# Attention scores computed transposed and turned in 32x32 blocks on VectorE, in batches 1 to 7 of a three-part kernel

## The chip, the core and the metric

The kernel runs on one core of a Trainium2 chip. The metric is device time in microseconds (us) of one execution; the time of the kernel before is the median of three runs. TensorE does the matrix products, VectorE (DVE in the rows) and ScalarE (ACT) the work on elements, GpSimd (POOL) some reductions and stores, SyncE (SP) issues most transfers.

## The reference

An attention against 32 memory slots for each head, and two feed-forward layers one after the other. Eight batches of 8 heads, 576 tokens, head size 64; then 4608 tokens of width 512, inner width 2048.

```python
a = softmax(phi, axis=2)                              # over the 576 tokens
k_m = einsum('bhsm,bhsd->bhmd', a, k)
v_m = einsum('bhsm,bhsd->bhmd', a, v)
attn = softmax(q @ k_m.transpose / sqrt(64), axis=-1) # over the 32 slots
x = (attn @ v_m), heads side by side                  # 4608 x 512
h = x @ w_in;   x = (h * sigmoid(h)) @ w_out
h = x @ w_in2;  x = elu(h) @ w_out2
```

## The kernel before

The kernel has two halves in time. In the first, batch after batch of 576 tokens goes through attention and the first layer; in the second, nine blocks of 512 tokens go through the second layer. Products of the two layers run in float16, each operand split into a high and a low half (`split_hi` on ScalarE, `split_lo` on VectorE, lines 170 to 177) and multiplied in three terms (`mm3`). Everything up to the attention weights is float32.

For one batch, `plan_mem` makes `k_m` and `v_m` (tiles `phi`, `eT`, `es`, `kvp`, `kvTp`, `kT`), `plan_u` multiplies `v_m` into the first weight matrix (`up`, `u`), and `plan_attn` makes the attention weights in three pieces j: 256, 256 and 64 tokens. For a piece of 256 tokens `scores` (L776) issues 16 matmuls with 64 tokens of `q` as weights and 64 columns of `kT` moving, tokens on the partitions of PSUM tile `sc`; `tile_position` puts them on the left or right 64 columns of the array. `att_max` and `att_sub` (VectorE, L793, L800) subtract the maximum over 32 slots, `att_exp` (ScalarE) takes the exponential, `att_sum` and `att_mul` (VectorE) divide by the sum. `att_T` (TensorE, L829) transposes the weights into PSUM tile `aTp`, slots on the partitions, and `att_split` brings them as a high and a low half into `aT`. The sixteen products of in1 (`plan_in1`, PSUM tile `ph` from `aT` and `u`) read `aT`; the seven products of out1 (`plan_out1`, `ph` from `T` and `w1s`) read operand splits `T` that VectorE and ScalarE make from the activations `h` (`plan_moving`). Conversions of the second layer's weights (`quad`, `raw`, `hl_q`) are spread over batches 2 to 7.

Batch 0 runs in an order written out by hand (`FIRST`); from batch 1 on a planner (`Plan`) sets the order: each step has an engine, an estimated cost, a rank or due time and the steps that it depends on, and each engine's list is filled by rank and readiness. Each engine then works through its list strictly in order. Attention of batch n + 1 is planned beside in1 and out1 of batch n. `sc` and `aTp` share a ring of two PSUM tiles (`A = "a", 2`), the weights `att` have two SBUF tiles.

Of the kernel before, what the change touches and what calls it, by code (L numbers as in the profile page):

```python
# [10 lines left out]
F32 = mybir.dt.float32  # L11
# [3 lines left out]
AF = mybir.ActivationFunctionType  # L15
ALU = mybir.AluOpType
AX = mybir.AxisListType
PSUM = bass.MemoryType.PSUM

P = 128  # L20
B, H, S, D, M = 8, 8, 576, 64, 32
DM, DFF = 512, 2048
NG = 2
NP = 4
NC = 5
TAIL = 64
# [51 lines left out]
def act(n, scaled=True):  # L78

    return (0.25 if scaled else 0.19) + n / 1165  # L80


def dve(n, fast=False):

    return 0.155 + n / (1920 if fast else 915)
# [7 lines left out]
def attn_moe_moe(ctx: ExitStack, tc: tile.TileContext, qT, phiT, kvm, kvt, w1i, w1o, w2i, w2o, out):  # L93
# [24 lines left out]
    def a_tile(shape, name, tag="a"):  # L118

        k = turn[0] % 4  # L120
        turn[0] += turn[1]
        if turn[1]:
            tag = "aauc"[k]
        return ps_a.tile(shape, F32, tag=tag, name=name, bufs=2 if tag == "a" else 1)
# [4 lines left out]
    def small(name, n=1):  # L129
        return sml.tile([P, n], F32, tag=f"s{n}", name=name, bufs={1: 10, 16: 6}.get(n, 2))  # L130
# [4 lines left out]
    def tt(out, a, b, op):  # L135
        nc.vector.tensor_tensor(out=out, in0=a, in1=b, op=op)  # L136
# [635 lines left out]
    def tokens(j):  # L772

        return (P, 2) if j < 2 else (TAIL, 1)

    def scores(b, j):  # L776
        z = st[b]
        r, n = tokens(j)
        ps = z["sc", j] = a_tile([P, 2, H, M], "sc")
        for c in range(2 * n if j < 2 else 1):  # L780
            t0 = 256 * j + 64 * c
            o = 64 * (c % 2)
            for p in range(NP):
                nc.tensor.matmul(  # L784
                    ps[o:o + 64, c // 2, 2 * p:2 * p + 2],
                    z["q", p][:, t0:t0 + 64],
                    z["kT"][:, p // 2, 64 * (p % 2):64 * (p % 2) + 64],
                    start=True,
                    stop=True,
                    tile_position=(0, o),  # L790
                )

    def att_max(b, j):  # L793
        z = st[b]
        r, n = tokens(j)
        sc = z["sc", j][:r, :n].rearrange("p n h m -> p (n h) m")
        z["smx", j] = small("smx", 16)
        nc.vector.tensor_reduce(out=z["smx", j][:r, :n * H], in_=sc, axis=AX.X, op=ALU.max)

    def att_sub(b, j):  # L800
        z = st[b]
        r, n = tokens(j)
        k = n * H
        sc = z.pop(("sc", j))[:r, :n].rearrange("p n h m -> p (n h) m")
        a = z["att", j] = two.tile([P, 16, M], F32, tag="att", name="att")
        tt(a[:r, :k], sc, z.pop(("smx", j))[:r, :k].unsqueeze(2).to_broadcast([r, k, M]), ALU.subtract)

    def att_exp(b, j):
        r, n = tokens(j)
        a = st[b]["att", j][:r, :n * H]  # L810
        nc.scalar.activation(out=a, in_=a, func=AF.Exp, scale=float(1.0 / np.sqrt(D)))

    def att_sum(b, j):
        r, n = tokens(j)
        k = n * H
        aa = st[b]["att", j][:r, :k]
        s1, s2 = small("ss1", 16), small("ss2", 16)
        st[b]["ss3", j] = small("ss3", 16)
        nc.vector.tensor_reduce(out=s1[:r, :k], in_=aa, axis=AX.X, op=ALU.add)
        nc.vector.tensor_scalar_add(s2[:r, :k], s1[:r, :k], 1e-9)  # L820
        nc.vector.reciprocal(st[b]["ss3", j][:r, :k], s2[:r, :k])

    def att_mul(b, j):
        r, n = tokens(j)
        k = n * H
        aa = st[b]["att", j][:r, :k]
        tt(aa, aa, st[b].pop(("ss3", j))[:r, :k].unsqueeze(2).to_broadcast([r, k, M]), ALU.mult)

    def att_T(b, j):  # L829
        z = st[b]  # L830
        r, n = tokens(j)
        a = z.pop(("att", j)).rearrange("p (n g h) m -> p n g (h m)", n=2, g=NG)
        ps = z["aTp", j] = a_tile([P, NG, 256], "aTp")
        for g in range(NG):
            for c in range(n):
                nc.tensor.transpose(ps[:, g, P * c:P * c + r], a[:r, c, g], ident[:r, :r])  # L836

    def att_split(b, j, lo):
        z = st[b]
        r, n = tokens(j)  # L840
        if j == 0 and not lo:
            z["aT"] = big.tile([P, NG, S], F32, tag="aT", name=f"aT{b}", bufs=2) if b == 0 else big.tile(
                [P, 2, NG, S], F16, tag="aT", name=f"aT{b}", bufs=2)
        t = slice(256 * j, 256 * j + n * r)
        ps = z["aTp", j][:, :, :n * r]
        if b == 0:
            copy(f"A0{j}", z["aT"][:, :, t], ps)
        elif not lo:
            split_hi(z["aT"][:, 0, :, t], ps, SA)
        else:  # L850
            split_lo(z["aT"][:, 1, :, t], z["aT"][:, 0, :, t], ps, SA)
# [121 lines left out]
    def plan_attn(pl, n, r, mem, after):  # L973


        A = "a", 2

        def on(eng, cost, fn, deps):
            return pl.add(eng, cost, r, fn, deps)

        qs, q_frees = [], []
        for p in range(NP):
            if n > 1:
                qs.append(pl.load(295, r - 290, lambda p=p: load_q(n, p), pl.ring("q", NP), QLATE))
            q_frees.append(pl.take("q", qs[-1]) if n > 1 else pl.rings["q"][p][1])
        aT, exps = [], []
        for j in range(3):
            rows, w = tokens(j)
            k = 256 * w
            sc = on("PE", 1.8 if j < 2 else 0.5, lambda j=j: scores(n, j), [mem["kT"]] + qs + pl.ring(*A))  # L990
            free = pl.take("a", sc)
            mem["kT_free"].append(sc)
            for f in q_frees:
                f.append(sc)
            mx = on("DVE", dve(k), lambda j=j: att_max(n, j), [sc])
            t = on("DVE", dve(k), lambda j=j: att_sub(n, j), [mx] + pl.ring("att", 2))
            a_free = pl.take("att", t)
            free.append(t)
            t = on("ACT", act(k, False), lambda j=j: att_exp(n, j), [t] + after)
            exps.append(t)  # L1000
            t = on("DVE", dve(k) + 0.45, lambda j=j: att_sum(n, j), [t])
            t = on("DVE", dve(k), lambda j=j: att_mul(n, j), [t])
            t = on("PE", 0.6 if j < 2 else 0.3, lambda j=j: att_T(n, j), [t] + pl.ring(*A))
            a_free.append(t)
            free = pl.take("a", t)
            h = on("ACT", act(k, False), lambda j=j: att_split(n, j, False), [t] + (aT or pl.ring("aT", 2)))
            if j == 0:
                aT_free = pl.take("aT", h)
            t = on("DVE", dve(k), lambda j=j: att_split(n, j, True), [h])
            free.append(t)  # L1010
            aT.append(t)
        return {"aT": aT, "exps": exps, "aT_free": aT_free, "scales": mem["scales"]}
# [850 lines left out]
```

## Time and profile before

| | |
|---|---|
| three runs | 1386.82, 1390.85, 1391.38 us; median 1390.85 |
| the profiled execution, span from first to last instruction | 1390.1 us |
| TensorE busy | 1345.9 us, 97% |
| VectorE busy | 1130.3 us, 81% |
| ScalarE busy | 948.2 us, 68% |
| batches 1 to 7 on TensorE | about 117 to 700 us |
| second layer | about 700 to 1390 us |

The profile gives, for one execution, each engine's instructions with their start and length. Matmuls overlap in the array, so the length of a row of matmuls is longer than the time to the next row's start; what a step costs TensorE is read from the distance of starts. PE is TensorE's matmuls, PEld its weight loads. A float32 matmul leaves two records.

### The profile page before, as it was taken

To read this page: it belongs to the slowest core of one execution; us is meant where nothing else is said; L and a number is where in the kernel's file an instruction comes from. 1 tells how busy PE (TensorE), PEld (TensorE's weight loads), DVE (VectorE), ACT (ScalarE), POOL (GpSimd) and SP (SyncE) were. 2 spreads that over 40 slices of the span, in tenths; PEclk is the share of its full clock that TensorE was granted. 3 is DMA by queue.
4 is the path that set the end of the run, shared out by engine and by line. 5 is a ranking of instruction groups with operands and counts; after the bars stand their busy time and mean duration, and the time that the engine had idled before them with its cause. 6 is when DMAs were issued, how large, how long until landed. Compare 5 with 4: busy or idle time off the path is not lost.

```text
span 1390.1 us, 28629 instructions
## 1 busy us (share of the span) xinstructions
PE 1345.9 (97%) x12048; PEld 1091.0 (78%) x12048; DVE 1130.3 (81%) x1753; ACT 948.2 (68%) x1357; POOL 53.2 (4%) x85
## 2 busy tenths in 40 slices
PE   4999999999999999999999999999999999999998
PEld 2676677776767767676787888888888888888887
DVE  6888888796998979797869787888888787879784
ACT  3666784967868685786658675758676676768672
POOL 0000100010010000001000000000000000000000
PEclk8999999999999999999999999999999999999999
DMA  9556777368576647745394232333333241514220
GB/s 368 178 180 214 261 271 255 131 224 283 179 244 238 228 167 250 262 141 215 119 368 154 82 129 82 122 99 100 107 104 118 71 151 43 170 51 141 81 95 31
DMA packets 68800, 233.06 MB, mean 168 GB/s; under 512 B 9024, under 2 KB 15168, under 8 KB 64064
## 3 DMA queue, kind: packets, MB, share of 16 engines
q1 hardware_dynamic: 60288, 199.78, 42.4%
q0 software_dynamic: 8384, 31.46, 5.8%
q8 instruction: 94, 1.54, 0.5%
q14 instruction: 34, 0.28, 0.1%
HBM read 186.12 MB, written 40.89 MB: 163 GB/s over the span
## 4 chain that ended last, share of the span: by engine, by line
PE 84%; DMA 5%; issue 4%; DVE 3%; ACT 3%; POOL 0%; SPq 0%; ACTq 0%; POOLq 0%; DVEq 0%
PE ph L1029 28%; PE o L1029 23%; PE h2A L1029 13%; PE h2D L1029 9%; PE ph L1078 3%; DMA wi<-w2is 2%; PE up L869 2%; PE ph L1036 2%; PE sc L784 2%; PE kvp L688 1%; DMA kv<-in_kvm 1%; DMA w2is<-hl_q 1%; PE eT L665 0%; DMA raw<-in_w1o 0%; PE aTp L836 0%
## 5 line engine op out<-in xcount | busy, mean ns | idle before, releaser
L1029 PE MATMUL o<-t,wq 128*128 128x256 f16 x3024 | 358.3, 273 | 0.1
L1029 PEld LDWEIGHTS <-wi 128*128 128x128 f16 x3024 | 295.1, 98 | 46.4 <-DMA wi<-w2is 9.3
L1029 PEld LDWEIGHTS <-wq 128*128 128x128 f16 x3024 | 295.7, 98 | 34.7 <-issue 0.3
L1029 PE MATMUL ph<-T,w1s 128*128 128x288 f16 x2352 | 301.7, 287 | 0.2 <-DVE T L177 0.2
L1029 PEld LDWEIGHTS <-w1s 128*128 128x128 f16 x2352 | 225.9, 98 | 64.0 <-issue 7.7
L1029 PE MATMUL h2A<-xh,wi 128*128 128x256 f16 x1728 | 228.6, 273 | 8.9 <-DMA wi<-w2is 7.4
L1467 ACT ACTIVATE h<-h2A,inv 128x256 f32<-128x256 f32 x288 | 133.7, 468 | 141.6 <-PE h2A L1029 139.2
L1029 PE MATMUL ph<-aT,u 128*128 128x288 f16 x1344 | 176.5, 288 | 1.1 <-ACT h L1115 0.9
L177 DVE SCALAR_TENSOR_TENSOR t<-h,s_g,t 128x768 f16<-128x768 f32 (+1 forms) x144 | 163.9, 1146 | 14.2 <-ACT t L172 13.9
L1029 PE MATMUL h2D<-xh,wi 128*128 128x256 f16 x1296 | 172.9, 273 | 0.0
L1471 DVE SCALAR_TENSOR_TENSOR h<-h2D,inv,h 128x256 f32<-128x256 f32 x216 | 103.8, 482 | 81.0 <-PE h2D L1029 59.1
L1029 PEld LDWEIGHTS <-u 128*128 128x128 f16 x1344 | 127.7, 98 | 49.6 <-issue 18.4
L172 ACT ACTIVATE t<-h,s_g 128x768 f16<-128x768 f32 (+1 forms) x144 | 146.4, 1034 | 22.8 <-DVE h L136 11.5
L177 DVE SCALAR_TENSOR_TENSOR T<-h,c,T 128x1152 f16<-128x1152 f32 x98 | 137.2, 1413 | 20.0 <-ACT T L172 19.7
L136 DVE TENSOR_TENSOR h<-h 128x256 f32<-128x256 f32 (+1 forms) x302 | 129.5, 463 | 2.8
L172 ACT ACTIVATE T<-h,c 128x1152 f16<-128x1152 f32 x98 | 119.5, 1252 | 13.8 <-DVE h L136 10.3
L1115 ACT ACTIVATE h<-ph,inv 128x576 f32<-128x576 f32 x112 | 82.3, 738 | 24.1 <-PE ph L1029 23.0
L1509 DVE SCALAR_TENSOR_TENSOR h<-e,h 128x1024 f32<-128x1024 f32 x72 | 87.8, 1219 | 7.3 <-ACT e L1505 7.3
L1502 ACT ACTIVATE e<-h 128x1024 f32<-128x1024 f32 x72 | 75.5, 1049 | 8.8 <-DVE h L1471 8.8
L1505 ACT ACTIVATE e<-e 128x1024 f32<-128x1024 f32 x72 | 75.6, 1050 | 0.7
L1078 PE MATMUL ph<-h,w1o 128*128 128x288 f32 x256 | 66.5, 418 | 0.0
L136 DVE TENSOR_TENSOR h<-h,h 128x1152 f32<-128x1152 f32 x42 | 56.5, 1354 | 9.9 <-ACT h L1115 9.7
(183 smaller groups left out, 1272.5 us busy)
## 6 DMA issues: line engine op xcount, KB each, us to landing
w1s<-w1os SPq DMA_DIRECT2D x98, 512.0 KB, 4.6
wi<-w2is SPq DMA_DIRECT2D x56, 896.0 KB, 4.7
kv<-in_kvm SPq DMA_DIRECT2D x48, 256.0 KB, 5.3
q<-in_qT SPq DMA_DIRECT2D x32, 288.0 KB, 7.9
out<-ye SPq DMA_DIRECT2D x36, 256.0 KB, 2.0
raw<-in_w1i SPq DMA_DIRECT2D x8, 1024.0 KB, 11.4
raw<-in_w1o SPq DMA_DIRECT2D x8, 1024.0 KB, 4.9
raw<-in_w2i SPq DMA_DIRECT2D x8, 1024.0 KB, 6.9
```

The costliest lines, as they stand in the source:

```text
L136: nc.vector.tensor_tensor(out=out, in0=a, in1=b, op=op)
L172: nc.scalar.activation(out=hi, in_=x, func=AF.Copy, scale=s)
L177: nc.vector.scalar_tensor_tensor(out=lo, in0=x, scalar=s, in1=hi, op0=ALU.mult, op1=ALU.subtract)
L784: nc.tensor.matmul(ps[o:o + 64, c // 2, 2 * p:2 * p + 2], z["q", p][:, t0:t0 + 64], z["kT"][:, p // 2, 64 * (p % 2):64 * (p % 2) + 64], st ...
L1029: nc.tensor.matmul(o, w, x[:, c], start=first, stop=last, **how)
L1078: nc.tensor.matmul(z[d][1][t], wB[d][:, k], h[k // KQ][:, t, k % KQ], start=(k == 0), stop=(k == KF - 1))
L1115: nc.scalar.activation(out=h[m // KQ][:, :, m % KQ], in_=w.pop(m), func=AF.Silu, scale=z["inv1"][:, m // 4:m // 4 + 1])
L1467: nc.scalar.activation(out=w["x"][:, s], in_=w["A"], func=AF.Copy, scale=inv)
L1471: return pl.add("DVE", COST["add"], base, lambda: nc.vector.scalar_tensor_tensor(out=w["x"][:, s], in0=w["D"], scalar=inv, in1=w["x"][:, s ...
L1502: nc.scalar.activation(out=w["e"], in_=w["x"][:, B21:], func=AF.Relu, scale=-1.0)
L1505: nc.scalar.activation(out=w["e"], in_=w["e"], func=AF.Exp, scale=-1.0)
L1509: nc.vector.scalar_tensor_tensor(out=x, in0=w["e"], scalar=-1.0, in1=x, op0=ALU.add, op1=ALU.max)
```

## The change

Only batches 1 to 7 change. A new `scores_T` computes the scores with 64 columns of `kT` as weights and up to 256 tokens of `q` as moving columns, so that slots lie on the partitions of `sc`; the left and right half of the array alternate with every matmul. `att_turn` is one VectorE instruction that transposes every 32x32 block from PSUM into the SBUF tile `att`: tokens modulo 32 come to lie on the partitions, and the 32 slots of a head side by side. `att_sub_T`, `att_exp_T` and `att_norm_T` do the same softmax as before, now from SBUF. `att_back`, one VectorE instruction again, turns the blocks back into PSUM tile `aTp`, in which the weights have the layout that `att_T` gave them; `att_split` is as it was. The last piece of 64 tokens works on 128 partitions x 128 columns where it worked on 64 x 256. The costs that the planner is told change with the steps.

```diff
@@ -834,6 +834,62 @@
         for g in range(NG):
             for c in range(n):
                 nc.tensor.transpose(ps[:, g, P * c:P * c + r], a[:r, c, g], ident[:r, :r])
+
+    def scores_T(b, j):
+        z = st[b]
+        n = P * tokens(j)[1] if j < 2 else TAIL
+        ps = a_tile([P, NG * 256], "sc")[:, :NG * n]
+        z["sc", j] = ps
+        for g in range(NG):
+            for e in range(2):
+                o = 64 * e
+                nc.tensor.matmul(
+                    ps[o:o + 64, g * n:(g + 1) * n],
+                    z["kT"][:, g, o:o + 64],
+                    z["q", 2 * g + e][:, 256 * j:256 * j + n],
+                    start=True,
+                    stop=True,
+                    tile_position=(0, o),
+                )
+
+    def by_head(b, j):
+
+        return st[b]["att", j], st[b]["att", j].rearrange("p k m -> p (k m)")
+
+    def att_turn(b, j):
+        z = st[b]
+        ps = z.pop(("sc", j))
+        z["att", j] = two.tile([P, 16, M], F32, tag="att", name="att")[:, :ps.shape[1] // M]
+        nc.vector.transpose(out=by_head(b, j)[1], in_=ps)
+
+    def att_sub_T(b, j):
+        z = st[b]
+        a, _ = by_head(b, j)
+        k = a.shape[1]
+        mx = small("smx", 16)[:, :k]
+        nc.vector.tensor_reduce(out=mx, in_=a, axis=AX.X, op=ALU.max)
+        tt(a, a, mx.unsqueeze(2).to_broadcast([P, k, M]), ALU.subtract)
+
+    def att_exp_T(b, j):
+        a, _ = by_head(b, j)
+        nc.scalar.activation(out=a, in_=a, func=AF.Exp, scale=float(1.0 / np.sqrt(D)))
+
+    def att_norm_T(b, j):
+        a, _ = by_head(b, j)
+        k = a.shape[1]
+        s1, s2, s3 = small("ss1", 16)[:, :k], small("ss2", 16)[:, :k], small("ss3", 16)[:, :k]
+        nc.vector.tensor_reduce(out=s1, in_=a, axis=AX.X, op=ALU.add)
+        nc.vector.tensor_scalar_add(s2, s1, 1e-9)
+        nc.vector.reciprocal(s3, s2)
+        tt(a, a, s3.unsqueeze(2).to_broadcast([P, k, M]), ALU.mult)
+
+    def att_back(b, j):
+        z = st[b]
+        _, a = by_head(b, j)
+        z.pop(("att", j))
+        ps = a_tile([P, NG * 256], "aTp")[:, :a.shape[1]]
+        nc.vector.transpose(out=ps, in_=a)
+        z["aTp", j] = ps.rearrange("p (g t) -> p g t", g=NG)
 
     def att_split(b, j, lo):
         z = st[b]
@@ -986,21 +1042,20 @@
         aT, exps = [], []
         for j in range(3):
             rows, w = tokens(j)
-            k = 256 * w
-            sc = on("PE", 1.8 if j < 2 else 0.5, lambda j=j: scores(n, j), [mem["kT"]] + qs + pl.ring(*A))
+            k = 256 * w if j < 2 else P
+            sc = on("PE", 1.0 if j < 2 else 0.3, lambda j=j: scores_T(n, j), [mem["kT"]] + qs + pl.ring(*A))
             free = pl.take("a", sc)
             mem["kT_free"].append(sc)
             for f in q_frees:
                 f.append(sc)
-            mx = on("DVE", dve(k), lambda j=j: att_max(n, j), [sc])
-            t = on("DVE", dve(k), lambda j=j: att_sub(n, j), [mx] + pl.ring("att", 2))
+            t = on("DVE", dve(k), lambda j=j: att_turn(n, j), [sc] + pl.ring("att", 2))
             a_free = pl.take("att", t)
             free.append(t)
-            t = on("ACT", act(k, False), lambda j=j: att_exp(n, j), [t] + after)
+            t = on("DVE", 2 * dve(k), lambda j=j: att_sub_T(n, j), [t])
+            t = on("ACT", act(k, False), lambda j=j: att_exp_T(n, j), [t] + after)
             exps.append(t)
-            t = on("DVE", dve(k) + 0.45, lambda j=j: att_sum(n, j), [t])
-            t = on("DVE", dve(k), lambda j=j: att_mul(n, j), [t])
-            t = on("PE", 0.6 if j < 2 else 0.3, lambda j=j: att_T(n, j), [t] + pl.ring(*A))
+            t = on("DVE", 2 * dve(k) + 0.45, lambda j=j: att_norm_T(n, j), [t])
+            t = on("DVE", dve(k), lambda j=j: att_back(n, j), [t] + pl.ring(*A))
             a_free.append(t)
             free = pl.take("a", t)
             h = on("ACT", act(k, False), lambda j=j: att_split(n, j, False), [t] + (aT or pl.ring("aT", 2)))
```

The planner moves instructions accordingly. On TensorE, in batch 1, the end of the first piece of scores and the start of the second, with steps of batch 0's outer product (`ph`) between; before:

```order
L784 MATMUL sc<-kT_892,q_408 64x64
L784 MATMUL sc<-kT_892,q_410 64x64
L784 MATMUL sc<-kT_892,q_412 64x64
L784 MATMUL sc<-kT_892,q_414 64x64
L1078 MATMUL ph<-h_145,w1o_706 128x288 x16
L1078 MATMUL ph<-h_146,w1o_706 128x288 x16
L836 MATMUL aTp<-ident,att 128x128 x4
L784 MATMUL sc<-kT_892,q_408 64x64
```

and with the change, from the start of the first piece:

```order
L846 MATMUL sc<-q_408,kT_892 64x256
L846 MATMUL sc<-q_410,kT_892 64x256
L846 MATMUL sc<-q_412,kT_892 64x256
L846 MATMUL sc<-q_414,kT_892 64x256
L1133 MATMUL ph<-h_145,w1o_706 128x288 x16
L1133 MATMUL ph<-h_146,w1o_706 128x288 x16
L1133 MATMUL ph<-h_145,w1o_855 128x288 x8
L846 MATMUL sc<-q_408,kT_892 64x256
```

Sixteen matmuls became four, the transposes of `att` between the pieces are gone, and the second piece stands eight matmuls of the outer product later.

On VectorE, at the end of the attention for batch 5, where the last piece is normalised and its low half made (`aT`, 128x2x64); `u` and `y` are results of other products, `inv`, `pvw`, `rec`, `c` small constants; before:

```order
L819 TENSOR_REDUCE ss_5292<-att 64x8
L820 TENSOR_SCALAR ss_5293<-ss_5292 64x8
L821 RECIPROCAL ss_5294<-ss_5293 64x8
L177 SCALAR_TENSOR_TENSOR aT_5118<-aTp,aT_5118 128x2x256
L136 TENSOR_TENSOR att<-att,ss_5294 64x256
L1258 SCALAR_TENSOR_TENSOR y<-ph,io_4298,y 128x288 x2
L177 SCALAR_TENSOR_TENSOR u_5_5303<-up,u_5_5303 128x512
L736 TENSOR_SCALAR inv_5341<-p_w1i,p_v 128x4
L136 TENSOR_TENSOR pvw<-p_v,p_w1im 128x1
L167 RECIPROCAL rec<-pvw 128x1
L168 TENSOR_SCALAR c_5343<-rec 128x1
L177 SCALAR_TENSOR_TENSOR aT_5118<-aTp,aT_5118 128x2x64
```

and with the change, from the sum of the last piece on:

```order
L881 TENSOR_REDUCE ss_5183<-att 128x4
L882 TENSOR_SCALAR ss_5184<-ss_5183 128x4
L883 RECIPROCAL ss_5185<-ss_5184 128x4
L136 TENSOR_TENSOR att<-att,ss_5185 128x128
L177 SCALAR_TENSOR_TENSOR aT_4999<-aTp,aT_4999 128x2x256
L891 STREAM_TRANSPOSE aTp<-att 128x128
L177 SCALAR_TENSOR_TENSOR u_5_5163<-up,u_5_5163 128x512
L1313 SCALAR_TENSOR_TENSOR y<-ph,io_4215,y 128x288 x2
L177 SCALAR_TENSOR_TENSOR aT_4999<-aTp,aT_4999 128x2x64
L736 TENSOR_SCALAR inv_5227<-p_w1i,p_v 128x4
L136 TENSOR_TENSOR pvw<-p_v,p_w1im 128x1
L167 RECIPROCAL rec<-pvw 128x1
```

The second piece's `aT` and the turn back stand between the product with the reciprocal and the last piece's `aT`, and the constants now come behind that `aT`.

## Rows read from the trace of the kernel before

**Rows 1.** Busy time by stretches, out1 of batches 2 and 4: window, length, PE, PEld, DVE, ACT, POOL.

```profile
264.70:316.40 51.70, 51.70 (x499) 39.49 (x498) 48.70 (x67) 35.40 (x54) 4.97 (x6) 1.00 0.60 209
...
431.50:482.00 50.50, 50.50 (x474) 38.99 (x471) 46.92 (x67) 32.18 (x51) 2.08 (x2) 1.00 0.71 252
```

**Rows 2.** Timeline of PE, out1 of batch 4: start, length, operation, count, idle before.

```profile
446.91 1.54 PE L784 MATMUL sc<-kT,q 128*64 128x64 f32 x32
448.38 15.61 PE L1029 MATMUL ph<-T,w1s 128*128 128x288 f16 x126
...
472.09 0.60 PE L836 MATMUL aTp<-ident,att 128*128 128x128 f32 x4
472.62 0.68 PE L784 MATMUL sc<-kT,q 128*64 128x64 f32 x8
473.23 0.91 PE L1029 MATMUL ph<-T,w1s 128*128 128x288 f16 x6
...
481.29 0.34 PE L836 MATMUL aTp<-ident,att 64*128 64x64 f32 x2
481.57 0.61 PE L869 MATMUL up<-w1i_hl,vT 128*32 128x512 f16 x8
482.12 1.65 PE L1029 MATMUL ph<-aT,u 128*128 128x288 f16 x12
```

**Rows 3.** Timeline of PE: a float32 stream, and one `kvp` group with its successor.

```profile
117.32 15.79 PE L1078 MATMUL ph<-h,w1o 128*128 128x288 f32 x64
132.94 0.60 PE L836 MATMUL aTp<-ident,att 128*128 128x128 f32 x4
...
434.89 0.43 PE L688 MATMUL kvp<-kv,es 128*32 128x128 f32 x8
435.25 2.01 PE L1029 MATMUL ph<-T,w1s 128*128 128x288 f16 x15
```

**Rows 4.** Groups by form, DVE: count, then busy us, mean ns, idle before.

```profile
L329 DVE TENSOR_SCALAR quad<-quad 128x1024 f32<-128x1024 f32 x16 | 11.0, 688 | 5.1 <-ACT quad L320 5.1
...
L136 DVE TENSOR_TENSOR att<-sc,smx 128x512 f32<-128x512 f32 x16 | 11.1, 691 | 0.5
...
L798 DVE TENSOR_REDUCE smx<-sc 64x8 f32<-64x256 f32 x8 | 3.3, 412 | 1.8 <-PE sc L784 1.8
```

**Rows 5.** Timeline of DVE: low half of the third `aT` piece, batches 1 to 5, 7.

```profile
151.57 0.28 DVE L177 SCALAR_TENSOR_TENSOR aT<-aTp,aT 128x128 f16<-128x128 f32 x1
...
227.44 0.29 DVE L177 SCALAR_TENSOR_TENSOR aT<-aTp,aT 128x128 f16<-128x128 f32 x1
...
315.29 0.27 DVE L177 SCALAR_TENSOR_TENSOR aT<-aTp,aT 128x128 f16<-128x128 f32 x1
...
398.51 0.28 DVE L177 SCALAR_TENSOR_TENSOR aT<-aTp,aT 128x128 f16<-128x128 f32 x1
...
482.09 0.29 DVE L177 SCALAR_TENSOR_TENSOR aT<-aTp,aT 128x128 f16<-128x128 f32 x1
...
642.92 0.29 DVE L177 SCALAR_TENSOR_TENSOR aT<-aTp,aT 128x128 f16<-128x128 f32 x1
```

**Rows 6.** Timeline of PE: first in1 matmuls of batches 1 to 4, 7; a `kv` wait.

```profile
156.88 1.64 PE L1029 MATMUL ph<-aT,u 128*128 128x288 f16 x12
...
236.95 1.63 PE L1029 MATMUL ph<-aT,u 128*128 128x288 f16 x12
...
316.38 1.63 PE L1029 MATMUL ph<-aT,u 128*128 128x288 f16 x12
...
336.46 0.66 PE L688 MATMUL kvp<-kv,es 128*32 128x128 f32 x8 [2.47 <-DMA kv<-in_kvm]
...
402.12 1.64 PE L1029 MATMUL ph<-aT,u 128*128 128x288 f16 x12
...
644.35 3.10 PE L1029 MATMUL ph<-aT,u 128*128 128x288 f16 x24
```

## The prediction

> **What bounds the kernel now.** I read the busy time by stretches first. The kernel spends its first half on seven batches (1 to 7), each with an inner product (in1, matmuls `ph<-aT,u`) and an outer one (out1, `ph<-T,w1s`). While out1 of one batch runs, the attention of the next is made. In the two out1 stages shown TensorE is busy for all of the stretch, 51.70 of 51.70 us and 50.50 of 50.50, so TensorE's list sets the pace there; VectorE has 48.70 and 46.92 us of work in the same time and so only 3.0 and 3.6 us of idle time [rows 1]. ScalarE has 35.40 and 32.18 and is no second bound. So the reader is to see two things: a microsecond taken from TensorE in this stage is a microsecond of the kernel, as long as VectorE keeps up; and VectorE has hardly any room.
>
> Next, TensorE's list in order of time around one such stage [rows 2]. Starts follow each other without a hole, so what a piece costs is the distance to the next start and not its printed duration: scores of 256 tokens 446.91 to 448.38, 1.47 us; the last 64 tokens 472.62 to 473.23, 0.61; the transpose of attention weights 0.53 (472.09 to 472.62) and for the last piece 0.28.
>
> **The change, part by part.** *TensorE, taken away.* Each batch has two pieces of 256 tokens and one of 64: 2 x 1.47 + 0.61 + 2 x 0.53 + 0.28 = 4.89 us.
>
> *TensorE, added.* The same scores come as four matmuls for a piece (16 or 4 before), keys as weights and 256 tokens as moving columns. Each float32 matmul leaves two records in the trace, so 8 records for a piece. In a plain float32 stream 64 records of 288 columns take 117.32 to 132.94, 0.244 us each or 0.85 ns a column [rows 3]. 256 columns are thus 0.217 us: 1.74 for a piece if the two 64-column halves of the array work in turn, 0.87 if side by side. That halves can work side by side is seen in `kvp`, which changes its quarter of the array with every matmul: 8 records of 128 columns take 0.36 us [rows 3], against 0.87 in turn and 0.22 with all four side by side; it pays 0.14 over the latter. Before the change scores switch halves only after four matmuls, and gain little: 32 records of 64 columns take 1.47, in turn 1.74. After it they switch with every matmul, as `kvp` does, which is why I price them by that row: 0.87 + 0.14 = 1.01 a piece, and for the last piece, 8 x 0.054 / 2 + 0.14 = 0.36, I take 0.40, since the same size takes 0.61 today. Sum 2.42; saved per batch 4.89 - 2.42 = 2.47 us, in seven batches **17.3 us**. Bounds: no surplus, 1.96 (20.5 us in all); halves in turn, 2 x 1.74 + 0.61 = 4.09 (5.6 us in all).
>
> A rule speaks against the better price. The Trainium skill ("TensorE: Matmul & The Clock Gate", Part 3, What overlaps and what doesn't) says that matmuls start and end strictly in program order. By it the two records of one matmul, on the same half, would hold up the next, a piece would take five record times, 1.22 us, and the saving would be 14.4 us. The `kvp` row does not bear it out: five record times there would be 0.54 us, and it takes 0.36.
>
> *VectorE, added.* The trace has no turn of 32x32 blocks. The nearest rows are float32 operations on 512 columns from PSUM, 0.69 us [rows 4], so a piece of 256 tokens costs two turns (scores into SBUF, weights back into PSUM) of 0.69, and the last piece two on 128 columns, which cost 0.28 by the `aT` rows of that width [rows 5]. In return the last piece's maximum, subtraction, sum and product shrink from 256 columns on half the partitions (0.41, [rows 4]) to 128 on all, 0.28. Sum: 4 x 0.69 + 2 x 0.28 - 4 x 0.13 = **2.80 us a batch**. Bounds: half price, as an SBUF operation on 1024 columns has it (0.69, [rows 4]), 1.3; double price, 6.1. I take the middle because both reads and writes of PSUM at one column a step are what the 0.69 row shows. None of this is hidden in seven batches unless VectorE's idle time takes it in. ScalarE's exp of the last piece gets 0.1 shorter; it has room, nothing.
>
> *Moved.* The planner's list for VectorE keeps the same 14 operand splits a batch and lets weight conversions (`quad`) slip behind the attention chain; the order in the section on the change shows the end of that chain, where the third `aT` has moved ahead of the scale constants, and TensorE's list no longer holds a transpose between the pieces, so a piece of scores now waits for VectorE's turn back of the piece before, where it waited for a TensorE transpose. Queued behind a waiting turn on VectorE are the `T` splits of out1, which TensorE reads next. Loads on SP's queue are the same in number; single `q`, `kv` and `w1s` loads change places by a few. I price that at nothing, covered by three `kv` buffers; uncovered, it is one more hole like the 2.47 us wait for `kv` in batch 3 [rows 6].
>
> **What VectorE lets through.** In1 of a batch starts when the third piece of `aT` has its low half from VectorE. How long that lies before in1's first matmul is the slack: batch 1, 151.85 to 156.88, 5.0 us; batch 2, 227.73 to 236.95, 9.2; batch 3, 315.56 to 316.38, 0.8; batch 4, 3.3; batch 5, 482.38 against 482.12, none; batch 7, 643.21 to 644.35, 1.1 [rows 2, 5, 6]; batch 6 I take like 4. TensorE comes 2.47 us sooner and VectorE has 2.80 more to do, so 5.27 us must come from slack and from VectorE's 3.3 us of idle time a stage [rows 1]. That idle time is mostly waiting for ScalarE's high halves, which will be ready when VectorE is later; I let between half and all of it be used. All of it: batch 3 is short by 1.2, 5 by 2.0, 7 by 0.9, the rest by nothing, 4.1 us. Half: 2.8, 3.6, 2.5 and 0.3 each in 4 and 6, 9.5 us. TensorE waits that long, newly, for `aT` or a late `T`. Middle: 6.8.
>
> **Sum.** 17.3 - 6.8 = 10.5 us less. The profiled execution has a span of 1390.1, from which 1379.6 is left; the median of the runs is 0.75 above that span, so **1380.4 us**, with its own range 1377.6 to 1383.1. About 0.3% (4.2 us) is what a measurement of this kernel can tell from no change.
>
> **The rivals.** *A, all of it arrives:* the planner lets enough conversion work slip that `aT` and `T` are never late: 1390.85 - 17.3 = 1373.5. For it: VectorE's order puts `aT` ahead of constants; against: slack of 0.8 and none in batches 3 and 5 [rows 2, 5, 6]. 15%.
>
> *B, VectorE takes the place of TensorE:* its waits for ScalarE stay, so no idle time is used. Short by 0.3, 0, 4.5, 2.0, 5.3, 2.0 and 4.2 in the seven batches, 18.3 against 17.3: 1391.9, no difference to be told. For it: the 93 to 94% busy share [rows 1]; against: a wait for a ScalarE result shrinks when the waiting side is late. 12%.
>
> *C, the turns are dear, slower:* a 32x32 turn of 4-byte data at twice the price of a copy, 1.38 us for 512 columns, in the attention chain of every batch. Then 2.47 + 6.1 = 8.57 us must be found; half the idle used, the batches are short by 1.9, 0, 6.1, 3.6, 6.9, 3.6 and 5.8, 27.9 us in all, and the kernel takes 1390.85 + 10.6 = 1401.5. It decides from where shortages pass 17.3, at about 1.0 us a turn (five batches, 4.8 turns' worth each, 7.8 us above the 9.5). For it: no row shows a turn, and it writes PSUM, which VectorE does nowhere in this trace; against: every single-price row of this width lies at 0.69. 15%.
>
> *D, the halves do not work side by side:* the piece costs 1.74, TensorE saves 0.80 a batch, 3.60 must be found, the batches 3, 5 and 7 are short by 1.2, 1.9 and 0.9, and 5.6 - 4.0 = 1.6 us are left: 1389.2. For it: scores before gain only 0.27 of 1.74 from switching; against: `kvp`. 8%.
>
> **How the numbers follow.** The forecast gets 50%. Faster by over 0.3%: forecast and A, 0.65; within: B and D, 0.20; slower: C, 0.15. The range reaches from A to B, 1373 to 1392, and leaves out C.
>
> **What would show it.** Right: `sc` pieces of 8 records about 1.0 us from start to next start, no `aTp` matmuls in batches 1 to 7, turns near 0.69, VectorE near 50 us busy of a 49 to 51 us out1 stage, and new TensorE waits for VectorE's `aT` or `T` in batches 3, 5 and 7 of some 7 us in all. Wrong: turns of 1 us and more with waits in every batch (C), pieces of 1.7 us (D), waits of 15 us and more at single price (B), or hardly any waits (A). A new wait for `kv` loads, or a second half of the kernel that is not the same length, would be a cause that I have not priced.

## The result, and the profile after

The change made the kernel slower: median 1403.07 us of four runs (1400.63 to 1406.30) against 1390.92 of four runs of the kernel before, ratio 1.0089, 95% interval 1.0067 to 1.0111, 12 us. 1380.4 with a range of 1373 to 1392 was predicted, and the result lies outside that range. The profiled execution, the fastest of the four, has a span of 1398.9 us against 1390.1, 8.8 longer. The changed kernel's lines stand 55 or 56 below those of before: `mm3` is L1084, the addition to `y` L1313.

What the change was to do it did. In the timeline of PE (start, length, operation, count) a piece of 256 tokens takes 274.65 to 275.67, 1.02 us, and the last piece 145.38 to 145.77, 0.39 [rows 2 had 1.47 and 0.61]:

```profile
145.38 0.45 PE L846 MATMUL sc<-q,kT 128*64 128x64 f32 x8
145.77 0.61 PE L925 MATMUL up<-w1i_hl,vT 128*32 128x512 f16 x8
...
274.65 1.08 PE L846 MATMUL sc<-q,kT 128*64 128x256 f32 x8
275.67 16.71 PE L1084 MATMUL ph<-T,w1s 128*128 128x288 f16 x135
```

The turns cost what other VectorE work of their width costs, from PSUM and into PSUM alike (groups by form, DVE: count, then busy us, mean ns, idle before; compare [rows 4]):

```profile
L891 DVE STREAM_TRANSPOSE aTp<-att 128x512 f32<-128x512 f32 x14 | 10.1, 720 | 0.2
...
L863 DVE STREAM_TRANSPOSE att<-sc 128x512 f32<-128x512 f32 x14 | 9.9, 710 | 3.0 <-PE sc L846 3.0
...
L891 DVE STREAM_TRANSPOSE aTp<-att 128x128 f32<-128x128 f32 x7 | 2.3, 325 | 0.2
...
L863 DVE STREAM_TRANSPOSE att<-sc 128x128 f32<-128x128 f32 x7 | 2.2, 313 | 5.4 <-PE sc L846 5.4
```

What is new are TensorE's waits. First the out1 stages of batches 2 and 4 (window, length, then PE, PEld, DVE, ACT, POOL, granted clock, DMA share, GB/s), which answer to [rows 1]:

```profile
259.59:314.94 55.35, 52.02 (x442) 37.48 (x439) 50.86 (x68) 33.38 (x52) 3.94 (x6) 0.94 0.54 184
...
434.47:486.86 52.39, 49.56 (x443) 36.59 (x440) 49.44 (x70) 33.55 (x55) 2.08 (x2) 1.00 0.75 260
```

TensorE no longer fills its stages, and they are longer: 55.35 where 51.6 had been enough. The view of TensorE's waits between 117 and 700 us (for whom; us in total, times, longest) says for whom:

```profile
PE ph L1084 <- DVE y L1313: 12.8, 6, 3.8
PE ph L1084 <- ACT h L1170: 4.7, 5, 1.6
PE up L925 <- DVE u L177: 3.6, 4, 1.6
PE ph L1084 <- DVE T L177: 2.3, 4, 1.6
PE up L925 <- DVE vT L177: 1.1, 1, 1.1
PE kvp L688 <- DMA kv<-in_kvm: 1.0, 2, 0.7
```

With two more of 0.8 us together these are 26.3 us; before the change the same view had 6.6 (4.2 of them for `kv`), so 19.7 are new. The largest are waits for the additions to `y`, VectorE instructions that read a PSUM bank of out1 before TensorE may write it again.

And the waits have a price of their own. Four windows, each from the end of one of the four longest waits:

```profile
301.98:310.00 8.02, 8.02 (x51) 5.00 (x51) 5.89 (x14) 2.20 (x5) 0.00 (x0) 0.63 0.48 172
393.01:400.00 6.99, 6.99 (x55) 4.33 (x55) 5.48 (x12) 2.27 (x5) 0.00 (x0) 0.76 0.18 53
557.62:565.00 7.38, 7.38 (x59) 4.44 (x60) 5.93 (x15) 2.95 (x6) 0.09 (x1) 0.81 0.75 273
639.12:645.00 5.88, 5.88 (x55) 3.98 (x55) 5.53 (x10) 3.09 (x5) 0.00 (x0) 1.00 0.36 137
```

After waits of 3.33, 3.82 and 2.95 us the granted clock was 0.63, 0.76 and 0.81, means over time at 1.2 and at 2.4 GHz; after the fourth, 2.09 us, it stayed at 1.00. (1 - 0.63) x 8.02 + (1 - 0.76) x 6.99 + (1 - 0.81) x 7.38 = 6.0 us of TensorE's time. The Trainium skill ("TensorE: Matmul & The Clock Gate", Part 1, HAM oscillation — how this bites in real kernels) describes this: waits that come round again and again leave the array at half its clock each time work resumes. Three of the four windows agree, the fourth does not. Both kernels have one more fall, between 332 and 345, with a clock of 0.87 over these 13 us in each, so that it drops out of the comparison.

Sum for the seven batches: 2 x 1.02 + 0.39 = 2.43 us a batch in place of 4.89, 17.2 less; 19.7 more waits; 6.0 for the clock: 8.5 more. The second layer's first matmul comes at 715.1 us where it came at 709.2, only 5.9 later. What lies between the two is found ahead of batch 1, in code that is the same in both kernels. The first scores of batch 1 start at 115.85 before and at 112.48 after, 3.4 us earlier. In both traces TensorE had just waited 3.45 us for ScalarE's `pad`; behind that wait the clock was 0.62 before and 1.00 after, which is 2.7 of the 3.4 us (timeline of PE and window behind the wait, before and then after):

```profile
108.72 1.11 PE L753 MATMUL kvTp<-ident,pad 128*128 128x128 f32 x4 [3.45 <-ACT pad L180]
108.72:115.85 7.13, 7.13 (x21) 5.20 (x21) 7.00 (x8) 2.88 (x4) 0.35 (x1) 0.62 1.03 332
```

```profile
108.01 0.66 PE L753 MATMUL kvTp<-ident,pad 128*128 128x128 f32 x4 [3.46 <-ACT pad L180]
108.01:112.48 4.47, 4.47 (x20) 3.35 (x20) 4.37 (x6) 2.57 (x3) 0.00 (x0) 1.00 1.02 332
```

That is chance between executions and no work of the change: in a second trace of the changed kernel the clock behind this wait, 3.85 us there, was 0.64, and in the kernel before with other lists (planner told measured costs) it stayed at 1.00 behind 3.31 us. From the first scores of batch 1 to the second layer it is 593.4 us before and 602.6 after, 9.3 more, against the 8.5 of the sum; 0.8 us stay open. That second trace (the last run of the table below) bears the sum out: 17.2 less, 20.8 more waits and 3.4 more for the clock (5.1 us less 1.7 before, as 1 - clock times length over stretches of 4 us) are 7.0 more, and the same stretch took 7.5 more.

The second layer itself took 2.9 us longer. Part of that are its waits for `wi` loads, the longest now 2.5 us; behind one of 1.95 us, which ended at 1051, the clock was 0.66 for 5 us. TensorE's waits for these loads from 700 us on, before and then after:

```profile
PE h2A L1029 <- DMA wi<-w2is: 7.4, 7, 1.4
```

```profile
PE h2A L1084 <- DMA wi<-w2is: 8.7, 7, 2.5
```

### The profile page after: what moved, and what is told of

It reads as the page before. It is cut to its first block, busy times and chain, and to the rows that moved or that the text cites. A ratio compares the mean times of both kernels' runs of the same rounds, so it can differ in the third digit from the quotient of the medians.

```text
span 1398.9 us, 27852 instructions
## 1 busy us (share of the span) xinstructions
PE 1334.5 (95%) x11642; PEld 1071.3 (77%) x11642; DVE 1147.9 (82%) x1795; ACT 945.2 (68%) x1357; POOL 50.0 (4%) x85
## 4 chain that ended last, share of the span: by engine, by line
PE 75%; DVE 11%; DMA 5%; issue 5%; ACT 4%; POOL 0%; ACTq 0%; SPq 0%; POOLq 0%; DVEq 0%
PE ph L1084 25%; PE o L1084 23%; PE h2A L1084 13%; PE h2D L1084 9%; DMA wi<-w2is 2%; DVE hl_q L177 2%; PE up L925 1%; PE ph L1091 1%; DVE att L136 1%; PE kvp L688 1%; PE sc L846 1%; DVE T L177 1%; DMA w1i_hl<-w1i_hl 1%; ACT T L172 1%; DMA x2d<-y 1%
## 5 line engine op out<-in xcount | busy, mean ns | idle before, releaser
L1084 PE MATMUL o<-t,wq 128*128 128x256 f16 x3024 | 358.8, 273 | 0.1
L1084 PEld LDWEIGHTS <-wi 128*128 128x128 f16 x3024 | 295.7, 98 | 48.2 <-DMA wi<-w2is 10.9
L1084 PEld LDWEIGHTS <-wq 128*128 128x128 f16 x3024 | 296.1, 98 | 34.9 <-issue 0.3
L1084 PE MATMUL ph<-T,w1s 128*128 128x288 f16 x2352 | 305.3, 289 | 14.9 <-DVE y L1313 12.6
L1084 PEld LDWEIGHTS <-w1s 128*128 128x128 f16 x2352 | 228.3, 99 | 85.6 <-issue 28.6
L1084 PE MATMUL h2A<-xh,wi 128*128 128x256 f16 x1728 | 229.4, 273 | 9.9 <-DMA wi<-w2is 8.7
L1084 PE MATMUL ph<-aT,u 128*128 128x288 f16 x1344 | 176.1, 287 | 5.5 <-ACT h L1170 4.7
L1084 PE MATMUL h2D<-xh,wi 128*128 128x256 f16 x1296 | 173.4, 273 | 0.0
L1084 PEld LDWEIGHTS <-u 128*128 128x128 f16 x1344 | 127.9, 98 | 55.1 <-issue 23.3
```

The costliest lines, as they stand in the source:

```text
L1084: nc.tensor.matmul(o, w, x[:, c], start=first, stop=last, **how)
```

## The experiments

Two theories stood at the start. V: VectorE's added time takes what TensorE saves. O: VectorE has the time, but the planner's new lists put its work in a bad order. Ratios are to the kernel before, measured beside each run, with 95% intervals.

| run | median us | ratio |
|---|---|---|
| change without maximum and subtraction | 1389.17 | 0.9990 [0.9973, 1.0007] |
| before, 19.3 us more VectorE, told to the planner | 1398.65 | 1.0049 [1.0035, 1.0064] |
| change, additions to `y` first | 1406.47 | 1.0109 [1.0080, 1.0137] |
| change in batches 1 and 2 alone | 1389.08 | 0.9984 [0.9969, 0.9999] |
| before, score matmuls alternating halves | 1385.88 | 0.9962 [0.9949, 0.9976] |
| change, 16 sums on GpSimd | 1425.65 | 1.0255 [1.0240, 1.0271] |
| before, planner told measured costs | 1396.64 | 1.0053 [1.0033, 1.0073] |
| before without maximum and subtraction | 1389.37 | 0.9984 [0.9964, 1.0003] |
| change's work in the old lists | 1405.83 | 1.0101 [1.0083, 1.0119] |
| before, 19.3 us more VectorE, old lists | 1400.36 | 1.0069 [1.0052, 1.0085] |
| old lists, without maximum and subtraction | 1383.11 | 0.9947 [0.9928, 0.9966] |
| old lists, scores issued twice | 1398.38 | 1.0064 [1.0045, 1.0083] |
| change, scores issued twice | 1410.63 | 1.0133 [1.0111, 1.0154] |
| change again, beside the last | 1402.86 | 1.0082 [1.0060, 1.0104] |

**Less VectorE in the change, more in the kernel before.** The first run drops a step, the second adds two instructions to `att_mul`:

```diff
-            t = on("DVE", 2 * dve(k), lambda j=j: att_sub_T(n, j), [t])
```

```diff
-            t = on("DVE", dve(k), lambda j=j: att_mul(n, j), [t])
+            t = on("DVE", (3 if j < 2 else 1) * dve(k), lambda j=j: (att_mul(n, j), att_extra(n, j)), [t])
...
+    def att_extra(b, j):
+        a = st[b]["att", j]
+        for i in range(2 if j < 2 else 0):
+            tt(a, a, a, ALU.max)
```

> The changed kernel without the maximum over the 32 slots and its subtraction (this part of the softmax is left out). Two theories of the 12 us that the change lost. V, VectorE's time: the change's saving on TensorE is real (17.3 us) and is eaten because VectorE has no room for 17.6 us more. O, the order: VectorE has the room, but its list has the two additions to y, which free the PSUM bank that out1 writes next, behind steps of the softmax. Here VectorE loses 14 x (0.685 + 0.692) + 7 x (0.286 + 0.292) = 23.3 us in seven batches and ends some 6 us under the kernel before. V: the whole saving comes out, 1390.9 - 17 = 1374 (1370 to 1379), waits for y under 3 us in all. O: the list still has the additions behind the rest of the softmax, so half or more of the 12.8 us of waits and of the fallen clock stays: 1384 or more.

> The kernel before with two more VectorE instructions of 128 x 512 behind the product with the reciprocal in each 256-token piece (the maximum of the weights with themselves, which alters nothing), and their cost told to the planner: 7 x 4 x 0.69 = 19.3 us more VectorE, TensorE's work as before. V: VectorE sets the pace of batches 2 to 7, so the time is that of the changed kernel or above it, 1401 to 1412, with waits of TensorE for y, u or aT of 10 us or more. O: VectorE has the room, 1391 to 1396.

Neither came out clean. Without the maximum the waits for `y` fell from 12.8 to 0.2 us, as V says, but 14 us came back and not 29: TensorE now waited 11.3 us for ScalarE's `h`, with one wait of 4.9 where ScalarE stood 6.7 us for the store of converted weights, whose buffer it needed (ScalarE's waits for transfers):

```profile
ACT hl_q L172 <- DMA w2is<-hl_q: 6.7, 1, 6.7
ACT y L363 <- DMA x2d<-y: 3.8, 1, 3.8
```

More VectorE in the kernel before cost 7 us, between the two theories.

**The order alone.**

```diff
+            pl.soon[t] = 30
-            self.tasks = [(t[0], t[1], latest[i], *t[3:]) for i, t in enumerate(self.tasks)]
+            self.tasks = [(t[0], t[1], latest[i] - self.soon.get(i, 0.0), *t[3:]) for i, t in enumerate(self.tasks)]
```

> The changed kernel with the additions to y due 30 us earlier in the planner, so that VectorE takes them as soon as the product they read is done; nothing else is altered. V: the waits for y go (under 3 us of the 12.8), and as much or more turns up in waits for u, aT or T, since VectorE has no less to do: 1399 to 1410. O: the 12.8 us and the clock that falls after them come back: 1383 to 1389.

1406.5, as V said: no wait for `y` is left, and 10.7 us for `T`, 5.3 for `vT`, 4.4 for `kv` and 5.7 for `h` stand in its place. But lists are not worth nothing:

```diff
-            sc = on("PE", 1.8 if j < 2 else 0.5, lambda j=j: scores(n, j), [mem["kT"]] + qs + pl.ring(*A))
+            sc = on("PE", 1.47 if j < 2 else 0.61, lambda j=j: scores(n, j), [mem["kT"]] + qs + pl.ring(*A))
...
-            t = on("PE", 0.6 if j < 2 else 0.3, lambda j=j: att_T(n, j), [t] + pl.ring(*A))
+            t = on("PE", 0.53 if j < 2 else 0.28, lambda j=j: att_T(n, j), [t] + pl.ring(*A))
```

> The kernel before with the same work, and the planner told what the score pieces and transposes took in the trace (1.47, 0.61, 0.53 and 0.28 us in place of 1.8, 0.5, 0.6 and 0.3): only the order of the lists moves. L, the order by itself is worth several us, because the lists of before fit its own costs: 1394 to 1402. V, order is worth little and VectorE's time much: 1389 to 1393.

The same work in other lists cost 5 us by the medians (1.0053), as O said (L in that expectation). So a run that changes what the planner is told can carry a difference of this size that has nothing to do with the work, and the decision needs runs with the same lists.

**The change's work in the old lists.** The planner is told the old steps and costs, and calls the new functions in their places:

```diff
-            mx = on("DVE", dve(k), lambda j=j: att_max(n, j), [sc])
-            t = on("DVE", dve(k), lambda j=j: att_sub(n, j), [mx] + pl.ring("att", 2))
+            mx = on("DVE", dve(k), lambda j=j: att_turn(n, j), [sc])
+            t = on("DVE", dve(k), lambda j=j: att_sub_T(n, j), [mx] + pl.ring("att", 2))
...
-            t = on("PE", 0.6 if j < 2 else 0.3, lambda j=j: att_T(n, j), [t] + pl.ring(*A))
+            t = on("PE", 0.6 if j < 2 else 0.3, lambda j=j: att_back(n, j), [t] + pl.ring(*A))
```

> The work of the change, instruction for instruction, in the lists of the kernel before: the planner is told the old steps with their old costs, the turn stands where the maximum stood, the turn back is issued where TensorE's transpose stood, and every other instruction of every engine keeps its place. O, the order: the change's work is a gain and its new lists lost it, so TensorE's 17.3 us come out less the 6 to 7 us that VectorE is short of: 1373 to 1384. V, VectorE's time: 17.6 us more have no room wherever they stand, 1396 to 1406, with waits for y, T or aT of 12 us or more. Between 1385 and 1395 both have a share.

> The kernel before with the same 19.3 us more VectorE in its attention as in the earlier run (1398.7), but not told to the planner, so that all lists are those of before. O: most of those 7.5 us were new lists, so 1390 to 1394. V: the VectorE time itself cost them, 1397 to 1405, with waits of TensorE for VectorE of 5 us or more.

> As the run of the change's work in the old lists, and without the maximum and its subtraction (left out of the softmax in batches 1 to 7): TensorE 17.3 us less and VectorE some 6 us less than before, order as before. O and V both give nearly the whole of TensorE's saving, 1373 to 1377. 1382 or more would mean that a third party, ScalarE's h or a load, holds TensorE once it comes early.

This decides against O: the time goes with VectorE's work and not with the lists. In the lists of before the change's work takes 1405.8, no less than in its own lists. Taking 23.3 us off VectorE in these lists (the third run; TensorE's work the same) takes 22.7 us off the kernel. TensorE's waits from 117 to 710 us, with the change's work and then without the maximum:

```profile
PE up L930 <- DVE vT L177: 6.9, 4, 2.3
PE ph L1090 <- DVE y L1319: 6.6, 3, 2.8
PE sc L846 <- DVE aT L177: 2.7, 3, 1.2
PE kvp L688 <- DMA kv<-in_kvm: 2.3, 1, 2.3
PE up L930 <- DVE u L177: 2.1, 4, 0.9
```

```profile
PE kvp L688 <- DMA kv<-in_kvm: 5.2, 2, 4.2
PE ph L1090 <- DVE y L1319: 2.7, 2, 2.5
PE up L930 <- DVE vT L177: 1.7, 1, 1.7
```

The third run also shows what holds TensorE once VectorE doesn't: one `kv` load of 4.2 us, and 8 us of the 17 came out. With TensorE as before, 19.3 us more VectorE cost 9 us, about half. TensorE's waits in that run are longest at its transposes, for `att`, the very weights whose making the two instructions lengthen:

```profile
PE aTp L841 <- DVE att L136: 9.0, 8, 2.4
```

And 24 us less (1130.3 to 1106.2 busy) gained nothing that can be told from no change:

> The kernel before without the maximum and its subtraction in batches 1 to 7 (ScalarE's exponential reads the scores from PSUM; this part of the softmax is left out): some 25 us less VectorE, TensorE as before. It is the partner of the changed kernel without the maximum (1389.2). V: before, VectorE was not the limit, so little comes out: 1386 to 1391, and TensorE's 17 us that the changed kernel saves beside it show as nothing more than 0 to 2 us. Rival, VectorE already held the kernel before: 1376 to 1384.

So before the change VectorE's results came just in time; the change made them later and TensorE earlier. What is full are stretches of VectorE's list, and not the engine: with the change's work in the old lists it still idles 81.6 us between 117 and 710, where it idled 89.1 before.

One rival is left. All these runs add or take VectorE's work inside the attention chain (scores to `aT`), so they do not tell the amount of work in VectorE's list from the length of that chain. The waits for `vT`, `y` and `u`, which are not made in the chain, speak for the amount; the 9.0 us for `att` speak for the chain. The run that was to take other work off VectorE (below) gave it no time back.

**Is TensorE's time still worth anything?** Then what TensorE saves should count only where VectorE keeps up.

> The kernel before with one loop turned round: the 16 score matmuls of a 256-token piece go to the left and right half of the array by turns, where eight went to one half and then eight to the other. No cost told to the planner and no other list changes. If the halves run side by side, as in the changed kernel (a piece 1.0 us), a piece falls from 1.47 to 0.8 to 1.1 us, some 0.4 us x 2 x 8 batches = 6.5 us. P, TensorE's time counts as long as VectorE's list is left alone: 1383 to 1386. N, TensorE arrives early and waits for the others whatever is saved on it: 1388 to 1391, with new waits of 4 us or more. If the halves don't run side by side with 64 columns each: piece and time as before.

(Before, the loop in `scores` changes halves after every four matmuls; the eight of this expectation are a slip.)

```diff
-        for c in range(2 * n if j < 2 else 1):
+        for c0, p, e in ([(c0, p, e) for c0 in (0, 2) for p in range(NP) for e in range(2)] if j < 2 else [(0, p, 0) for p in range(NP)]):
+            c = c0 + e
```

```profile
291.74 1.15 PE L785 MATMUL sc<-kT,q 128*64 128x64 f32 x32
292.83 1.40 PE L1030 MATMUL ph<-T,w1s 128*128 128x288 f16 x10
```

A piece takes 1.09 us (291.74 to 292.83), 0.38 less, which is 6 us over eight batches, and 5.3 us (0.38%) came out: this version beats both kernels, without one instruction more on VectorE. With the full change the saving is worth less than nothing in the old lists:

```diff
-            for e in range(2):
+            for e in (0, 1, 0, 1):
```

> The run of the change's work in the old lists (1405.8), with every score matmul of batches 1 to 7 issued twice, the second writing the same result over the first: TensorE gets 2 x 1.0 + 0.4 us a batch more to do, 17 us in all, which is what the change took from it; VectorE's work and all lists stay. If VectorE sets the pace and TensorE's early arrival only turns into waits, after which the granted clock falls (0.62 to 0.75 in eleven stretches of 5 us in that run, in none of the run with VectorE's time added to the kernel before, 1400.4): the waits of 2 us and more go, the clock stays up and the time falls to 1398 to 1402 although more is done. If the clock has no part and VectorE sets the pace alone: 1404 to 1407. If TensorE's time counts here: 1412 to 1423.

17 us more for TensorE made it faster, 1.0064 against 1.0101 (each by the kernel before on its own chip; the intervals just touch). Waits fell from 22.9 to 10.7 us, the mean granted clock of the run rose from 0.982 to 0.992. (Of the eleven stretches of 5 us in which the expectation finds a lowered clock, eight lie at 0.62 to 0.75 and three at 0.84 to 0.94.) In the run without doubled scores the clock fell also after smaller holes than the three above: windows before and after holes of 0.47 and 1.51 us near 223 and 225, and of 1.22 and 1.68 near 309 and 311:

```profile
217.00:222.00 5.00, 5.00 (x43) 4.01 (x41) 4.88 (x9) 4.72 (x6) 1.16 (x1) 1.00 0.80 274
...
225.00:232.00 7.00, 6.54 (x47) 4.24 (x48) 5.98 (x15) 3.07 (x6) 0.00 (x0) 0.76 0.36 135
305.00:310.00 5.00, 3.79 (x31) 2.79 (x29) 4.78 (x13) 2.14 (x3) 1.36 (x1) 1.00 0.75 282
...
312.00:320.00 8.00, 7.86 (x48) 4.71 (x49) 7.57 (x15) 2.79 (x6) 0.73 (x1) 0.63 0.23 86
```

In the change's own lists it is not so:

> The changed kernel itself, in its own lists, with every score matmul of batches 1 to 7 issued twice, 17 us more for TensorE in all; measured on one chip beside the changed kernel as it is. If VectorE sets the pace and the waits' clock is part of the loss: waits of TensorE in batches 1 to 7 fall from 26 us to under 18, the stretches at a granted clock of 0.6 to 0.8 from five to one or two, and the time stays or falls, 1394 to 1403. If TensorE's time counted in these lists: 1412 to 1420. If neither waits nor clock change: 1403, as the changed kernel.

> The changed kernel as it is, beside the one above on the same chip: 1400 to 1406 by its earlier runs (ratio 1.0089).

A miss: 1410.6 against 1402.9 on one chip, so 17 us more for TensorE cost 8. Its waits fell only from 27 to 23 us; the clock came back in part, as expected: what it cost in the batches, over stretches of 4 us as above, went from 5.1 to 3.6 us. The view of VectorE's waits shows why, the changed kernel first and the doubled one second:

```profile
DVE att L863 <- PE sc L846: 8.4, 8, 1.9
```

```profile
DVE att L863 <- PE sc L846: 13.9, 11, 2.2
```

In these lists VectorE stands at `att_turn` for scores that come late in TensorE's list, while TensorE stands for an addition that comes later in VectorE's. The two wait for each other by turns, and work on either engine counts by about a half: 8 of 17 us more on TensorE here, 14 of 23 us less on VectorE in the first run. In the old lists with the change's work VectorE never waits for scores.

**Room on VectorE.** Two runs tried to keep the change where VectorE can bear it.

> The change in the attention of batches 1 and 2 alone, batches 3 to 7 as before. In the changed kernel out1 of batch 1, where attention of batch 2 runs, took 49.37 us where it had taken 52.29, and the conversions of the second layer's weights had hardly begun. V: with room on VectorE the saving comes out in both, 2 x 2.5 = 5 us: 1384 to 1388. O: the same here or better; a time of 1390 or more would speak against both, since the saving itself would then be in doubt.

```diff
+        def new_of(n, j):
+            return n <= 2
```

1389.1, a gain of 2 us of the 5 that V expected, too near to nothing, and with new lists, to carry a reading.

> The changed kernel with the 16 sums of the second layer's weights (128 x 1024, 1.22 us each) on GpSimd in place of VectorE: 19.5 us less VectorE in batches 2 to 7, output unchanged. V, VectorE's time is what the change paid with: the waits for y fall from 12.8 us to under 4, and as in the run without the maximum some 12 us come back, 1388 to 1394. L, the time hangs on how the planner's lists happen to fall, and any change reshuffles them: 1396 to 1405, with waits of other names. If GpSimd is slow at such sums, the hl_q steps and stores behind them come late, and ScalarE, which works on hl_q between the activations h, holds TensorE in in1: 1398 or more.

```diff
-            return pl.add("DVE", dve(1024), 0, lambda: tt(t[out], t[a], t[b], op), deps)
+            return pl.add("POOL", 2.6, 0, lambda: nc.gpsimd.tensor_tensor(out=t[out], in0=t[a], in1=t[b], op=op), deps)
```

The third reading: a sum takes 2.78 us on GpSimd, ScalarE stood 28.8 us for the results, and behind it TensorE 16.8 us for `h`. It says nothing on V, since VectorE did not get the time back (below).

## Why the prediction was wrong

**Right.** The piece of scores, 1.02 us for 1.01 predicted, and 0.39 for 0.40; so 17.2 us for 17.3 saved on TensorE. The halves work side by side, and rival D is out. The turn, 0.71 and 0.72 for 0.69, which takes rival C out; that the price holds for writing PSUM too was a guess that came true, since the row of 0.69 reads PSUM and writes SBUF. VectorE's whole added time, 1147.9 - 1130.3 = 17.6 us of busy time for 7 x 2.80 = 19.6.

Two sums in it are off, without weight for the forecast. Five record times were put at 1.22 us with the 0.244 of a record of 288 columns; a record of 256 takes 0.217, which gives 1.09 (16.2 us saved), only 0.07 above the piece measured. So the piece alone hardly speaks against the strict order that the Trainium skill states ("TensorE: Matmul & The Clock Gate", Part 3, What overlaps and what doesn't); the `kvp` row, 0.36 for 0.54, does so more clearly. And the lower bound of VectorE's added time, at half price, is 1.1 and not 1.3.

**Wrong: the step "What VectorE lets through".** It took 6.8 us off the saving, from 4.1 to 9.5; measured are 19.7 us of new waits. It failed in two places.

First, it took one product of VectorE, the third piece of `aT`, and read its slack before in1 as VectorE's slack. In1 waited 0.5 us for `aT` in all. The waits fell on steps in the middle of out1, where slack was never looked up. The addition to `y` in batch 2, in the timeline of DVE of the kernel before:

```profile
303.43 0.94 DVE L1258 SCALAR_TENSOR_TENSOR y<-ph,io,y 128x288 f32<-128x288 f32 x2
```

It ended at 304.37, 39.6 us into out1 of batch 2 (from 264.76). TensorE needed it, with 288 records of out1 issued, at 306.13, so the slack was 1.8 us:

```profile
306.13 0.54 PE L1029 MATMUL ph<-T,w1s 128*128 128x288 f16 x3
```

In the changed kernel TensorE came to the same place, again after 288 records, at 298.65, 39.1 us into its stage (from 259.59) and 2.3 us sooner, and VectorE had the addition done at 301.83, 42.2 us into it and 2.6 us later: 2.3 + 2.6 - 1.8 leaves 3.1 of a wait of 3.33, in the timelines of PE and of DVE. VectorE had no gap in these 8 us:

```profile
293.33 5.32 PE L1084 MATMUL ph<-T,w1s 128*128 128x288 f16 x42
301.98 3.04 PE L1084 MATMUL ph<-T,w1s 128*128 128x288 f16 x12 [3.33 <-DVE y L1313]
```

```profile
293.44 0.72 DVE L863 STREAM_TRANSPOSE att<-sc 128x512 f32<-128x512 f32 x1 [1.13 <-PE sc L846]
...
299.65 0.69 DVE L136 TENSOR_TENSOR att<-att,ss 128x512 f32<-128x512 f32 x1
...
300.90 0.93 DVE L1313 SCALAR_TENSOR_TENSOR y<-ph,io,y 128x288 f32<-128x288 f32 x2
```

Second, it let half to all of VectorE's idle time be used. Of its waits for ScalarE's `T` half was: they fell from 19.7 to 9.6 us in the batches. But a new wait of 8.4 us, for scores, took the place of most of it.

Rival B, "VectorE takes the place of TensorE", was nearest, by the prediction's own sign (waits of 15 us and more at single price). That its waits, 18.3 us, were nearly right is luck: they were worked out from the slack of `aT` before in1 and from waits for ScalarE that stay, and neither is what happened. It was given 12%, and the time that it gave, 1391.9, was still 11 us short.

**Not priced: the clock and the second layer.** The granted clock does not stand in the prediction at all. Its 6.0 us, the 1.4 us by which the waits exceed rival B's, and the 2.9 us of the second layer make 1391.9 + 10.3 = 1402.2, where 1403.1 was measured; since falls of the clock differ between executions (the two traces of the changed kernel lost 8.5 and 5.1 us to it in the batches, that of before 1.7), this is no exact account. The loads, priced at nothing, gained 3.2 us in the batches (`kv` from 4.2 to 1.0; 3.1 in the second trace) and lost 1.3 in the second layer.

**The sign.** The chance for slower, 15%, came from rival C, dear turns, alone. That VectorE at its ordinary price would also cost TensorE's clock was no case of its own.

## What to carry to other kernels

Here, moving work from the bound engine to one that is 93 to 94% busy in the same stage moved the bound; take slack from every result that the bound engine waits for (buffer releases in the middle of a stage above all), and take the earlier arrival of the faster engine off that slack too. Price the holes of TensorE by the clock behind them as well as by their length, and as a chance, since the same hole lowered the clock in one trace and not in another. Before a reordering planner's new lists are blamed or praised, run the new work in the old lists: here those runs told work from order, and the part of the change that asks nothing of VectorE, alternating the halves, was the part worth keeping.

## What the runs showed of the hardware

The granted clock fell after single holes of TensorE of 2.95, 3.33 and 3.82 us in the changed kernel's batches, after one of 2.47 us in the kernel before (336.46; 0.73 for the 5.5 us behind it), after one of 1.95 in the second layer, and, with the change's work in the old lists, after two of 0.5 and 1.5 us close together. It did not fall after one of 2.09 at 639, nor after one of 3.46 at 108 in the changed kernel, where the same hole lowered it in the trace of before. So the length of a hole alone does not tell whether the clock falls. The falls behind the first three holes cost 1.4 to 3.0 us each.

With sums on GpSimd, VectorE lost 19.5 us of work and was as busy as before, 1147.5 us for 1147.9: instructions with two SBUF inputs grew (subtraction of the maximum, 692 to 791 ns on average), the turns, which read or write PSUM, did not (710 to 711):

```profile
L136 DVE TENSOR_TENSOR att<-att,smx 128x512 f32<-128x512 f32 x14 | 11.1, 791 | 0.5
...
L863 DVE STREAM_TRANSPOSE att<-sc 128x512 f32<-128x512 f32 x14 | 10.0, 711 | 2.4 <-PE sc L846 2.4
```

The Trainium skill ("SBUF — State Buffer", SBUF: two separate sides) has the rule for it: a GpSimd instruction that reads SBUF and a VectorE instruction with two SBUF inputs shut each other out. The two rows agree with it.
